# Two transposes of y moved from TensorE to transposing DMAs, and three stores to another queue, in a linear-attention and channel-mix kernel

## The chip, the core and the metric

The kernel runs on one core of a Trainium2 chip. The metric is the device time of one execution in microseconds; for several runs it is their median. The kernel's order of instructions is written out by hand, so each engine works through a fixed list.

## The reference

For each of 8 batches and 8 heads, with 576 tokens and 64 columns a head, linear attention without a mask is computed and normed, and its output goes through a channel mix with a shift by one token:

```python
kv = np.einsum('bhsd,bhse->bhde', k, v)
out = np.einsum('bhsd,bhde->bhse', q, kv)
rms = np.sqrt(np.mean(out * out, axis=-1, keepdims=True) + 1e-06)
x = (out / rms * g_norm)            # heads side by side: [8, 576, 512]
...
x_prev = np.concatenate([zeros, x[:, :-1, :]], axis=1)
xk = mu_k * x + (1.0 - mu_k) * x_prev
xr = mu_r * x + (1.0 - mu_r) * x_prev
k = np.maximum(xk @ w_k, 0.0)       # 512 -> 1024
v = k * k @ w_v                     # 1024 -> 512
r = 1.0 / (1.0 + np.exp(-(xr @ w_r)))
return (r * v)
```

Inputs and output are float32; the kernel works in bfloat16 with float32 sums.

## The kernel before, in words

Batches are counted from 0 in the code (a or b = 0 to 7); batch seven is a = 6, batch eight a = 7. The work of a batch is cut into small steps, each a short word in ORDER (lines 18 to 110), and the words are run in that order. A word names a step and its arguments: `K.6.5.1'=0` is step K for batch 6, chunk 5, half 1; a stroke puts its copy on DVE in place of ScalarE; the digits behind the equals sign are the PSUM banks that it takes. A bank is free again when the instruction that reads it last has been written down in the order. Each engine runs its own instructions in the order of the words and waits only for what they need. ORDER has eight periods; period p holds mostly the channel mix of batch p and the attention of the next one or two.

The steps that matter here, in the order in which a batch a passes through them:

- `ld` (lines 189 to 194): POOL issues the load of q, k or v with a cast to bfloat16.
- `kv`, `kvo`, `kvs`: k times v on TensorE, copies of it to SBUF, and a copy with the partition halves swapped.
- `qd` (lines 302 to 305): from a = 4 on, one transposing DMA on SP's queue turns q, 18 blocks of 128x128. Before that `qt` turns q on TensorE.
- `u`: q times kv into PSUM, in three parts. `sq` (ScalarE), `red` and eight `nw` (DVE) make the reciprocal root of the mean square by two Newton steps.
- `mul` (lines 393 to 397): DVE multiplies u by it and writes y, tokens in partitions. Five per batch; part 2 is the first group of 64 tokens, which stands alone ("group zero").
- `x0` and `x` (lines 413 to 429): TensorE turns y in 4 and 32 pieces (line 411). `x0o` and `xo` (lines 419, 431) copy the result from PSUM to xT with the factor g (`move`, lines 399 to 403), two copies each. xT has two buffers, one for even and one for odd a; a row of it is 64 columns of the token before and then the 576 tokens, 640 columns for each of four head pairs.
- `wrap` (line 567) fills the 64 columns ahead of the tokens, since tokens stand in a permuted order of nine groups. `dif` (line 571) subtracts the shifted x, four `sc` per mix (lines 577 and 579) multiply by mu, two `add` per mix (line 594) give xk (`add.a.0`) and xr (`add.a.1`).
- `K` (lines 603 to 622): four matmuls of 288 columns on xk, then the relu copy to an rt buffer, of which there are seven. `ks` squares an rt buffer of both halves into sqk. 16 K and 8 ks per batch.
- `R` (lines 626 to 632): four matmuls of 512 columns on xr and a sigmoid on ScalarE. `V` (lines 634 to 640): the product with w_v for a tile of 128 tokens in two parts of four matmuls. Tiles are counted over a pair of batches, nine to a pair; `V.7.5` is tile 5 of the last pair.
- `fin` (lines 650 to 655): DVE multiplies the V product from PSUM by the sigmoid into one of seven output buffers, and both halves of 64 partitions are stored by two DMAs on SP's queue. The last tile, 8 of the last pair, is done in two halves of columns, `L.1` and `L.0` (lines 642 to 648); there the first store is on SP's queue and the second on ScalarE's.

A store or a transposing DMA waits, beside its data, until the transfer eight before it has landed, because eight semaphores go round. SP's queue holds the q transposes and all stores but two.

Of the kernel before, what the change touches and what calls it, by code (L numbers as in the profile page):

```python
# [45 lines left out]
    red.2.0.5 nw.2.0.1 ksp.1.1.0.2 ld.0.4 R.1.5=5 Kp.1.1.5=7 nw.2.1.2 nw.2.2.3 ksp.1.1.4.6 nw.2.3.4 nw.2.4.5
    nw.2.5.6 R.1.8=1 nw.2.6.7 nw.2.7.8 mul.2.1.0 Kp.1.1.7=5 mul.2.1.1 mul.2.2.0 mul.2.0.0 R.1.6=7 V.1.4.0=2
    x0.2=16 mul.2.0.1 x0o.2.1 x0o.2.0 ksp.1.1.6.8 qt.3.1=35 kv.3=74 x.2.0.4=61 V.1.5.0=0 xo.2.0.4.0' xo.2.0.4.1
    V.1.5.1 ld.1.4 wrap.2 V.1.4.1 dif.2 kvo.3.1 V.1.7.0=6 sc.2.0.1' sc.2.0.0' sc.2.0.2 sc.2.0.3 sc.2.1.0
    add.2.0.0 sc.2.1.2' V.1.7.1 V.1.6.0=1 sc.2.1.3' qto.3.1.1 add.2.0.1 V.1.6.1 kvo.3.0'  # L50
# [13 lines left out]
    K.3.4.0'=7 fin.2.0 sc.3.1.1 u.4.0=41 u.4.1=53 sc.3.1.2' sq.4.0.1 sq.4.1.0 ld.2.7 u.4.2=2 K.3.1.0=0 sq.4.0.0
    add.3.1.0 sq.4.2.0 K.3.1.1'=7 K.3.5.1=6 red.4.5.9 K.3.0.1=0 K.3.5.0'=7 sq.4.1.1 red.4.0.5 K.3.3.1=6
    add.3.1.1 nw.4.0.1 nw.4.1.2 nw.4.2.3 K.3.0.0=0 K.3.2.0=7 kv.5=60 kvo.5.0 nw.4.3.4 nw.4.4.5 kvo.5.1 K.3.7.0=7
    nw.4.5.6 K.3.2.1=6 nw.4.6.7 ks.3.0 nw.4.7.8 kvs.5.1 mul.4.1.1 ks.3.2' R.3.7=0 mul.4.0.0 V.2.3.0=7 mul.4.2.0
    mul.4.0.1 ks.3.5 K.3.4.1=6 K.3.6.1=0 V.2.3.1 kvs.5.0' ks.3.1' ld.0.7 ks.3.4 K.3.7.1=3 K.3.3.0=6 mul.4.1.0
    R.3.6=4 K.3.6.0=2 ks.3.3 fin.2.3 x0.4=01 u.5.2=3 x0o.4.1' ks.3.7' x0o.4.0' ks.3.6 x.4.0.4=56 xo.4.0.4.1'
# [7 lines left out]
    K.4.3.1=5 mul.5.2.0 V.3.8.0=7 K.4.0.1=0 K.4.5.1=1 qd.6 sc.4.1.3' ks.4.3' add.4.1.1 ks.4.0 x.5.0.4=62
    xo.5.0.4.0 xo.5.0.4.1' kv.6=43 x0.5=50 K.4.5.0=1 add.4.1.0 wrap.5 kvo.6.1' K.4.2.0'=2 x0o.5.0 ks.4.7'
    x0o.5.1 ks.4.5' kvo.6.0 ks.4.2 R.4.1=6 K.4.6.1=3 kvs.6.1' R.4.0=1 dif.5 sc.5.0.1 sc.5.0.2 K.4.4.1=5 kvs.6.0
    K.4.4.0'=2 sc.5.0.3' sc.5.0.0 V.3.8.1 fin.3.8 sc.5.1.1' V.4.0.0=0 R.4.2=4 u.6.1=63 ks.4.6' sq.6.1.1 ks.4.4'  # L80
    add.5.0.1 add.5.0.0 u.6.2=1 sq.6.2.0 u.6.0=25 sq.6.0.0 V.4.0.1 fin.4.0 sq.6.0.1 qd.7 sq.6.1.0
    """,
    """
    K.5.7.0=7 R.4.3=4 K.5.5.1=0 K.5.3.1=7 red.6.5.9 red.6.0.5 nw.6.0.1 K.5.5.0=4 K.5.1.1=0 K.5.2.0=7 nw.6.1.2
    nw.6.2.3 nw.6.3.4 K.5.2.1=4 nw.6.4.5 nw.6.5.6 K.5.7.1'=0 K.5.1.0'=7 V.4.1.0=4 nw.6.6.7 K.5.4.1=0 nw.6.7.8
    mul.6.2.0 sc.5.1.0 V.4.1.1 mul.6.0.1 ks.5.1 mul.6.1.0 V.4.3.0=7 sc.5.1.2 x0.6=10 mul.6.0.0 mul.6.1.1
    sc.5.1.3' kv.7=56 ks.5.2' x0o.6.0' add.5.1.0 x0o.6.1' kvo.7.1 kvo.7.0 x.6.0.4=23 xo.6.0.4.1 add.5.1.1
    xo.6.0.4.0 kvs.7.0 wrap.6 K.5.0.0=6 dif.6 K.5.4.0=5 fin.4.1 kvs.7.1 K.5.6.1=1 sc.6.0.0' K.5.0.1'=0 K.5.6.0=3
# [16 lines left out]
    K.7.3.1'=2 V.6.2.1 V.6.3.0=6 V.6.0.0=4 fin.5.7 ks.7.3' fin.6.2 R.6.0=1 K.7.7.1=2 V.6.1.0=3 ks.7.7' fin.5.5
    K.7.5.1'=5 ks.7.1 K.7.0.1=1 R.6.3=2 K.7.6.1=7 fin.5.8 add.7.1.0 ks.7.2' ks.7.0 V.6.1.1 V.6.3.1 V.7.7.0=5
    sc.7.1.2 add.7.1.1 ks.7.5 fin.6.1 V.7.4.0=1 R.7.6=0 R.7.5=2 ks.7.6 R.7.7=7 V.7.6.0=3 R.7.4=0 fin.6.3 V.7.4.1
    V.6.0.1 V.7.5.0=6 fin.7.4 V.7.6.1 V.7.5.1 V.7.7.1 fin.6.0 R.7.8=2 fin.7.6 fin.7.5 fin.7.7 L.1=7 L.0=0 wm.1=1
# [10 lines left out]
def kernel(  # L119
# [272 lines left out]

    def mult(a, part, i):
        y, rs, (t0, n) = mine(a, "y", [128, NRG, NHP, HD], BF16), at[a]["rs"], TILES[part]
        g = rg(t0, n, i) if n else slice(0, 1)
        DVE.tensor_mul(out=y[:, g], in0=give(("u", a, part, i)),  # L396
                       in1=rs[:, g].unsqueeze(3).to_broadcast([128, max(n, 1), NHP, HD]))
# [252 lines left out]
    def finish(b, t, key, c=slice(0, C), queues=(nc.sync, nc.sync)):  # L650
        o = work.tile([128, c.stop - c.start], FP32, tag="out", name="out_sb", bufs=7)
        DVE.tensor_mul(out=o, in0=give(key), in1=sig[b, t][:, c])  # L652
        for i in range(2):
            bb, j = b - b % 2 + (2 * t + i) // G, (2 * t + i) % G
            queues[i].dma_start(out=out[bb].rearrange("(p j) c -> j p c", j=G)[j, :, c], in_=o[half(i), :])
# [35 lines left out]
    def part_square(b, j, f0, f1, eng):  # L691
# [101 lines left out]
```

## Time and profile before

| what | value |
|---|---|
| three runs of the kernel before | 202.69, 200.93, 203.99 us; median 202.69 |
| profiled execution, own time | 201.74 us |
| its span | 200.0 us |
| granted clock of TensorE | 0.997 |
| instructions in the span | 6027 |
| matmuls of line 411 (turning y) | 252, 6.4 us busy |
| HBM read and written | 33.56 MB and 9.44 MB |

The page of the profile gives busy times of each engine (PE is TensorE's matmuls, PEld its weight loads, DVE VectorE, ACT ScalarE, POOL GpSimd, SP SyncE, which issues DMAs), shares of the chain of work that ended last, and groups of instructions by line. "ps_x" is the PSUM tile of the turned y, "ps_km" that of K, "ps_r" of R, "ps_v" of V; "m" is the product with mu, "dx" the difference, "rt" the relu, "sqk" its square, "out_sb" an output buffer. In the views of one line, three numbers with strokes between them are the least, the median and the greatest duration in nanoseconds. A queue is written SPq or ACTq.

### The profile page before, as it was taken

The page shows a single profiled execution, that of the slowest core. Times are in us where ns is not written, and L with a number is a line of the kernel's source. Part 1 is how long each engine was busy: PE and PEld are TensorE (multiplying, and loading weights), DVE is VectorE, ACT ScalarE, POOL GpSimd, SP SyncE. Part 2 cuts the span into 40 slices and gives each one's busy share as a digit, 9 for nine tenths or more (in the row PEclk, how much of TensorE's full clock was granted, in tenths as well). Part 3 has the DMA queues.
Part 4 walks back from the last instruction along what each step waited for, and adds up shares of the span by engine and source line. Part 5 has one row for each costly group of instructions (what it writes and reads, how often), then busy time and mean ns, then how long its engine had stood idle before and what let it go on. Part 6 is the DMA issues. An engine that isn't in the chain of part 4 may idle for free.

```text
span 200.0 us, 6027 instructions
## 1 busy us (share of the span) xinstructions
PE 190.9 (95%) x2523; PEld 114.0 (57%) x2523; DVE 158.4 (79%) x344; ACT 140.3 (70%) x289; POOL 27.2 (14%) x44
## 2 busy tenths in 40 slices
PE   7789999999999999999999999999999999999990
PEld 2446744665455764476645665766565556554450
DVE  1499997998978999999999998898889973763250
ACT  3397975989956996788893899959986955075210
POOL 7854342003000400412000000000000000000000
PEclk9999999999999999999999999999999999999998
DMA  6999999999994899999999902530330020465284
GB/s 216 213 206 207 201 206 209 207 233 227 252 209 81 134 214 164 231 247 272 212 227 219 185 3 52 116 61 0 86 77 3 0 52 3 91 140 116 49 179 113
DMA packets 30767, 29.56 MB, mean 148 GB/s; under 512 B 11148, under 2 KB 25748, under 8 KB 30740
## 3 DMA queue, kind: packets, MB, share of 16 engines
q0 software_dynamic: 14912, 16.19, 48.6%
q1 hardware_dynamic: 15668, 12.85, 27.6%
q8 instruction: 20, 0.33, 0.6%
q10 hardware_dynamic: 160, 0.13, 0.2%
q14 instruction: 7, 0.06, 0.1%
HBM read 33.56 MB, written 9.44 MB: 215 GB/s over the span
## 4 chain that ended last, share of the span: by engine, by line
PE 88%; DMA 4%; DVE 2%; POOL 1%; issue 1%; ACT 1%; DVEq 0%; POOLq 0%
PE ps_v L639 30%; PE ps_km L607 29%; PE ps_r L629 16%; DMA rt<-in_v_dram 4%; PE ps_x L411 3%; PE ps_km L679 2%; PE ps_kv L290 2%; PE ps_u L319 2%; PE ps_qt L333 1%; PE ps_v L647 1%; PE ps_u L355 1%; PE ps_warm L264 1%; POOL q L183 1%; ACT sq L521 1%; DVE sqk L615 1%
## 5 line engine op out<-in xcount | busy, mean ns | idle before, releaser
L607 PE MATMUL ps_km<-xk,wk_sb 128*128 128x288 bf16 (+3 forms) x480 | 66.7, 285 | 0.0
L639 PE MATMUL ps_v<-wv_sb,sqk 128*128 128x512 bf16 x280 | 66.4, 379 | 0.3
L607 PEld LDWEIGHTS <-wk_sb 128*128 128x128 bf16 x480 | 45.4, 98 | 18.3 <-issue 0.2
L599 ACT ACTIVATE rt<-ps_km 128x288 bf16<-128x288 f32 (+3 forms) x87 | 35.9, 428 | 14.4 <-PE ps_km L607 12.3
L639 PEld LDWEIGHTS <-sqk 128*128 128x128 bf16 x280 | 26.7, 98 | 28.8 <-DVE sqk L615 0.4
L632 ACT ACTIVATE sig<-ps_r 128x512 bf16<-128x512 f32 x36 | 21.3, 596 | 21.3 <-PE ps_r L629 21.3
L629 PE MATMUL ps_r<-wr_sb,xr 128*128 128x512 bf16 x144 | 35.8, 379 | 0.0
L652 DVE TENSOR_TENSOR out_sb<-ps_v,sig 128x512 f32<-128x512 f32 (+1 forms) x37 | 24.6, 671 | 9.5 <-ACT sig L632 5.7
L577 ACT ACTIVATE m<-dx,cols 128x576 bf16<-128x576 bf16 (+1 forms) x34 | 24.8, 763 | 1.8 <-DVE dx L571 1.7
L613 ACT ACTIVATE sqk<-rt 128x576 bf16<-128x576 bf16 (+2 forms) x32 | 22.1, 710 | 0.1
L601 DVE TENSOR_SCALAR rt<-ps_km 128x288 bf16<-128x288 f32 (+3 forms) x33 | 15.4, 471 | 8.0 <-PE ps_km L607 7.8
L629 PEld LDWEIGHTS <-xr 128*128 128x128 bf16 x144 | 13.8, 98 | 13.3
L396 DVE TENSOR_TENSOR y<-ps_u,rs 128x512 bf16<-128x512 f32 (+1 forms) x30 | 17.2, 630 | 0.3
L364 DVE TENSOR_REDUCE ss<-sq 128x16 f32<-128x1024 bf16 (+1 forms) x12 | 15.9, 1346 | 0.3 <-ACT sq L360 0.3
L360 ACT ACTIVATE sq<-ps_u 128x512 bf16<-128x512 f32 (+1 forms) x30 | 14.4, 560 | 1.4 <-PE ps_u L319 1.4
L615 DVE TENSOR_TENSOR sqk<-rt 128x576 bf16<-128x576 bf16 (+4 forms) x25 | 12.4, 509 | 2.4 <-ACT rt L599 2.1
L594 DVE TENSOR_TENSOR xr<-m,xT 128x1152 bf16<-128x1152 bf16 x16 | 12.0, 751 | 1.7 <-ACT m L577 1.5
L401 ACT ACTIVATE xT<-ps_x,cols 128x1024 bf16<-128x1024 bf16 (+3 forms) x17 | 10.4, 648 | 3.5 <-PE ps_x L411 3.3
L571 DVE TENSOR_TENSOR dx<-xT 128x2304 bf16<-128x2304 bf16 (+5 forms) x13 | 11.6, 895 | 1.0 <-ACT xT L401 0.5
L594 DVE TENSOR_TENSOR xk<-m,xT 128x1152 bf16<-128x1152 bf16 (+2 forms) x16 | 10.8, 698 | 0.1
L579 DVE TENSOR_SCALAR m<-dx,cols 128x576 bf16<-128x576 bf16 (+3 forms) x32 | 10.4, 354 | 0.2
L403 DVE TENSOR_SCALAR xT<-ps_x,cols 128x128 bf16<-128x128 bf16 (+3 forms) x19 | 8.0, 438 | 2.1 <-PE ps_x L411 1.9
(87 smaller groups left out, 153.9 us busy)
## 6 DMA issues: line engine op xcount, KB each, us to landing
out_dram<-out_sb SPq DMA_DIRECT2D x70, 128.0 KB, 2.5
sq<-in_k_dram POOLq DMA_DIRECT2D x3, 576.0 KB, 14.6
qT<-in_v_dram POOLq DMA_DIRECT2D x3, 576.0 KB, 15.1
q<-in_q_dram POOLq DMA_DIRECT2D x3, 576.0 KB, 12.6
in_q<-in_q_dram POOLq DMA_DIRECT2D x3, 576.0 KB, 12.4
in_v<-in_v_dram POOLq DMA_DIRECT2D x3, 576.0 KB, 16.4
in_k<-in_k_dram POOLq DMA_DIRECT2D x3, 576.0 KB, 14.3
wk_sb<-in_moe_w_k_dram POOLq DMA_DIRECT2D x2, 512.0 KB, 9.8
```

Source lines behind the costliest of these rows:

```text
L364: DVE.tensor_reduce(out=ss[:, g0:g1], in_=sq[:, g0:g1], op=ALU.add, axis=AX.X)
L396: DVE.tensor_mul(out=y[:, g], in0=give(("u", a, part, i)), in1=rs[:, g].unsqueeze(3).to_broadcast([128, max(n, 1), NHP, HD]))
L577: eng.activation(out=out_, in_=in_, func=AF.Copy, scale=mu)
L594: DVE.tensor_add(out=dst, in0=m[:, hs, c0:c1], in1=x[:, hs, c0:c1])
L599: eng.activation(out=dst, in_=ps, func=AF.Relu)
L601: eng.tensor_scalar(out=dst, in0=ps, scalar1=0.0, scalar2=None, op0=ALU.max)
L607: nc.tensor.matmul(ps[:, n, :], wk_sb[:, cc, 128 * fc:128 * fc + 128], at[b]["xk"][:, cc, c0:c1], start=(cc == 0), stop=(cc == NHP - 1))
L613: eng.activation(out=sqk[:, fcs, o:o + n], in_=src, func=AF.Square)
L629: nc.tensor.matmul(ps, xr[:, cc, 128 * t:128 * t + 128], wr_sb[:, cc, :], start=(cc == 0), stop=(cc == NHP - 1))
L632: ACT.activation(out=sig[b, t], in_=give("r"), func=AF.Sigmoid)
L639: nc.tensor.matmul(ps, sqk[:, fc, 128 * t:128 * t + 128], wv_sb[:, fc, :], start=(fc == 0), stop=(fc == NFC - 1))
L652: DVE.tensor_mul(out=o, in0=give(key), in1=sig[b, t][:, c])
```

## The change

Three things are changed. First, for a = 6 and 7 `mul` writes into a new tile yd, four head pairs by five blocks of 128 columns, and `yd` turns the whole tile by one transposing DMA on SP's queue into xT, wrap columns included: 20 blocks of 128x128. One half of yd's first block is set to zero once at the start. The multiplication of group zero becomes two instructions of 64 partitions, since its rows are all written to the upper partition half. `x`, `x0`, `xo` and `x0o` are gone for these batches; `gx` multiplies xT by g in place, in two pieces of two head pairs, both on DVE. There is one yd tile, so the multiplications of a = 7 wait until yd.6 has read it.

Second, tiles 5, 6 and 7 of the last pair are finished by `fip`, which stores the first half on SP's queue, and `sta`, which stores the second on ScalarE's.

Third, all periods but the first are in a new order, with other PSUM banks, and some copies, squares and products with mu have changed between ScalarE and DVE. In it the q transposes qd.6 and qd.7 stand earlier among the stores of SP's queue.

```diff
+    YD = (6, 7)
+    yd = const.tile([128, NHP, 1 + NHP, 128], BF16, name="yd")
+
+    def mult_rows(a, part, i):
+
+        rs, (t0, n) = at[a]["rs"], TILES[part]
+        u_, pairs = give(("u", a, part, i)), yd.rearrange("p (c i) t x -> p c i t x", i=2)
+        if n:
+            by = rs[:, rg(t0, n, i)].unsqueeze(3).to_broadcast([128, n, NHP, HD])
+            DVE.tensor_mul(out=pairs[:, :, i, 1 + t0:1 + t0 + n].rearrange("p c t x -> p t c x"), in0=u_, in1=by)
+        else:
+            for h in range(2):
+                by = rs[half(h), 0].unsqueeze(2).to_broadcast([64, NHP, HD])
+                DVE.tensor_mul(out=pairs[half(1), :, h, 0], in0=u_[half(h), 0], in1=by)
+
+    DVE.memset(yd[half(0), :, 0], 0.0)
+
+    def y_turn(a):
+
+        nc.sync.dma_start_transpose(out=xT[a % 2].rearrange("p n (t x) -> p (n t) x", x=128), in_=yd.rearrange("p n t x -> p (n t x)"))
+
+    def by_g(a, hs, eng):
+        x = xT[a % 2][:, hs, P:]
+        move(eng, x, x)
+
     def mult(a, part, i):
+        if a in YD:
+            return mult_rows(a, part, i)
...
-        for i in range(2):
-            bb, j = b - b % 2 + (2 * t + i) // G, (2 * t + i) % G
-            queues[i].dma_start(out=out[bb].rearrange("(p j) c -> j p c", j=G)[j, :, c], in_=o[half(i), :])
+        for i, q_ in enumerate(queues):
+            store(b, t, i, q_, c)
...
+        "yd": lambda eng, a: y_turn(a),
+        "gx": lambda eng, a, h: by_g(a, heads[h], eng),
...
+        "fip": lambda eng, b, t: finish(b, t, ("v", b, t), queues=(nc.sync,)),
+        "sta": lambda eng, b, t: store(b, t, 1, nc.scalar),
```

The new order of the sixth period from its middle, of the seventh, and of the eighth:

```diff
...
+    K.5.0.1=0 mul.6.1.1 sc.5.1.2 V.4.3.0=3 V.4.3.1 K.5.6.0=0 K.5.1.0=6 K.5.0.0=5 mul.6.1.0 mul.6.0.1 sc.5.1.1
+    kv.7=72 mul.6.0.0 kvo.7.0 sc.5.1.0' K.5.5.1=0 K.5.3.1=1 K.5.6.1'=6 K.5.2.0'=5 add.5.1.0 ks.5.2 kvo.7.1
+    K.5.1.1'=7 V.4.1.1 kvs.7.1 kvs.7.0' yd.6 ks.5.1 add.5.1.1 fin.4.1 K.5.7.1=0 fin.4.3 K.5.3.0=1 ks.5.5'
+    ks.5.4' K.5.7.0'=6 ks.5.3' u.7.0=52 u.7.2=7 u.7.1=04 ks.5.7' R.5.8=1 sq.7.0.0 R.5.6=3 sq.7.1.1 R.4.2=6
+    gx.6.0' sq.7.0.1 V.4.2.0=1 V.4.2.1 gx.6.1' wrap.6 ks.5.0 dif.6 sq.7.1.0 sc.6.0.2 fin.4.2 R.5.4=3 R.5.5=6
+    sc.6.0.1' sq.7.2.0 sc.6.0.0' R.5.7=1 ks.5.6 sc.6.0.3' add.6.0.0 add.6.0.1 red.7.0.5 V.5.4.0=3
     """,
     """
+    K.6.1.1=6 red.7.5.9 nw.7.0.1 nw.7.1.2 K.6.7.1=1 sc.6.1.1 nw.7.2.3 nw.7.3.4 V.5.4.1 nw.7.4.5 K.6.0.1=6
+    nw.7.5.6 V.5.6.0=1 nw.7.6.7 nw.7.7.8 mul.7.0.1 mul.7.1.1 V.5.7.0=6 V.5.7.1 mul.7.1.0 mul.7.2.0 V.5.6.1
+    sc.6.1.2 K.6.6.0=2 mul.7.0.0 yd.7 V.5.8.0=4 K.6.5.1'=0 K.6.7.0'=7 sc.6.1.3 ks.6.7' add.6.1.1 sc.6.1.0
+    add.6.1.0 V.5.8.1 K.6.2.1=2 fin.5.4 K.6.6.1'=5 K.6.2.0'=0 K.6.0.0=7 K.6.4.0'=2 K.6.3.0=3 K.6.1.0=7 K.6.5.0=5
+    ks.6.2 fin.5.7 R.6.2=0 K.6.3.1'=2 ks.6.3 R.6.1=3 fin.5.8 gx.7.1' gx.7.0' ks.6.0 V.5.5.0=6 R.6.3=7 ks.6.1'
+    wrap.7 dif.7 sc.7.0.3' fin.5.6 K.6.4.1=5 V.6.1.0=0 V.5.5.1 sc.7.1.1' sc.7.0.0 V.6.3.0=2 R.6.0=4 sc.7.0.1'
+    ks.6.6 add.7.0.0 sc.7.0.2' sc.7.1.2 add.7.0.1 V.6.2.0=3 V.6.0.0=7
     """,
     """
+    K.7.3.1'=5 K.7.5.1=1 K.7.2.1'=4 ks.6.4' ks.6.5' K.7.0.1=5 K.7.1.1=1 sc.7.1.3' K.7.0.0=4 K.7.2.0'=5
+    K.7.7.1'=1 fin.5.5 sc.7.1.0 K.7.5.0=4 K.7.6.1'=5 add.7.1.0 ks.7.0 V.6.0.1 V.6.1.1 V.6.3.1 K.7.4.1=1 ks.7.5
...
+    fin.6.0 fin.6.3 ks.7.3 R.7.7=6 R.7.4=5 V.7.7.0=1 ks.7.7' V.7.4.0=4 V.7.7.1 R.7.6=3 R.7.8=6 fip.7.7 V.7.4.1
+    sta.7.7 fin.7.4 R.7.5=7 fin.6.1 V.7.5.0=2 V.7.6.0=5 V.7.6.1 fip.7.6 sta.7.6 V.7.5.1 fip.7.5 sta.7.5 L.1=1
+    L.0=3 wm.1=6
```

More of the change, by code (lines that the diff above doesn't have):

```diff
@@ L46 @@
[L46 to L50, printed above, removed]
@@ L65 @@
[L65 to L69, printed above, removed]
@@ L77 @@
[L77 to L81, printed above, removed]
@@ L82 @@
-    """,
-    """
[L84 to L88, printed above, removed]
@@ L105 @@
[L105 to L108, printed above, removed]
+    sc.1.1.0 sc.1.0.0.0.384 sc.1.0.3.0.384 fin.0.2 sc.1.0.2.0.384' Kp.1.0.0=5 Kp.1.0.2'=0 add.1.0.0.0.384
```

76 lines of the change are left out of this document (43 added, 33 removed).

## The prediction

> **What bounds the kernel now.** I read the page first (busy times, slices, shares of the chain), then the chain of work in order of time, then the windows by stretch, then the end of the timeline with the store queues, and last the transposing DMAs that the kernel already has.
>
> ```profile
> span 200.0 us, 6027 instructions
> ...
> PE 190.9 (95%) x2523; PEld 114.0 (57%) x2523; DVE 158.4 (79%) x344; ACT 140.3 (70%) x289; POOL 27.2 (14%) x44
> ...
> POOL 7854342003000400412000000000000000000000
> ...
> PE 88%; DMA 4%; DVE 2%; POOL 1%; issue 1%; ACT 1%; DVEq 0%; POOLq 0%
> ```
>
> ```profile
> 125.30:144.20 18.90, 18.90 (x286) 12.03 (x285) 17.70 (x38) 16.05 (x35) 0.00 (x0) 1.00 0.30 63
> 144.20:163.10 18.90, 18.90 (x150) 11.41 (x149) 15.98 (x33) 14.11 (x29) 0.00 (x0) 1.00 0.19 41
> ...
> sum 156.00, PE 156.00 PEld 94.55 DVE 129.57 ACT 113.95 POOL 8.89; mean PE 22.29 PEld 13.51 DVE 18.51 ACT 16.28 POOL 1.27
> ```
>
> The second fence is the windows view, from 38.3 to 194.3 us in seven stretches (two shown, and the sum of all; behind the stretch and its length stand PE, PEld, DVE, ACT and POOL busy, the granted clock, DMA share, GB/s). TensorE is busy in 156.00 of 156.00 us at a granted clock of 1.00. So nothing is gained before 194.3 by removing a wait; there is none. Only fewer matmuls shorten this part, and a new wait lengthens it. The first part, up to about 38 us, has the same order in both kernels.
>
> The chain of work (start, length, what) shows the matmuls that go, and the end:
>
> ```profile
> 133.64 0.17 PE ps_x L411 x4
> ...
> 134.51 0.57 PE ps_x L411 x32
> ...
> 154.76 0.63 PE ps_x L411 x36
> ...
> 155.99 0.86 PE ps_v L639 x4
> 156.85 0.49 PE ps_km L607 x4
> ...
> 192.56 1.76 PE ps_v L647 x16
> ...
> 194.34 0.42 DVE out_sb L652
> ```
>
> The last product of DVE is there at 194.76, yet the span is 200.0. The end of the timeline, and the stores that are issued after 194.9, show why:
>
> ```profile
> 188.19 8.66 SPq L655 DMA_DIRECT2D out_dram<-out_sb  x12
> 193.98 1.29 ACTq L655 DMA_DIRECT2D out_dram<-out_sb  x2
> ...
> L655 SPq DMA_DIRECT2D out_dram<-out_sb x3: 546/657/846, 194.6 to 196.3; - x3
> L655 ACTq DMA_DIRECT2D out_dram<-out_sb x1: 478/478/478, 194.8 to 194.8; - x1
> DMA to landing us min/median/max: 2.0/2.4/2.8
> ```
>
> SP issues twelve stores without a pause from 188.19 to 196.85, 0.72 us each. Both halves of the last tile's last part are made at 194.76; ScalarE issues its half at 194.8, SP its own only at 196.3. The end waits for SP's backlog of 1.5 us, then 2.0 us for the landing, then 1.7 us of closing.
>
> **The change part by part.** The profiled execution took 201.74 us, 1.74 beside its span of 200.0; the sum is made against it. The median of the three runs, 202.69, is 0.95 above it.
>
> 1. Matmuls. The transposes of y leave TensorE for batches seven and eight (a = 6 and 7): 0.17 + 0.57 and 0.63 us in the chain, 36 instructions each. That is -1.37 us, and since TensorE has no gap there, the following work moves up by all of it.
>
> 2. Each of these batches gets one transposing DMA of 20 blocks of 128x128 (yd.6, yd.7) on SP's queue. The kernel already turns q with four such DMAs of 18 blocks. Those two that run after the loads have ended, and the two before:
>
> ```profile
> L305 SPq DMA_TRANSPOSE qT<-q x1: 2823/2823/2823, 110.5 to 110.5; - x1
> L305 SPq DMA_TRANSPOSE qT<-in_q x1: 2818/2818/2818, 127.3 to 127.3; - x1
> DMA to landing us min/median/max: 4.7/4.7/4.7
> ...
> L305 SPq DMA_TRANSPOSE qT<-in_q x1: 4762/4762/4762, 79.6 to 79.6; - x1
> POOL q L194: 15.0, 1
> DMA to landing us min/median/max: 9.1/9.1/9.1
> ```
>
> Alone: 2.82 us of issue on SP, 4.7 to landing. Among the loads, around 67 to 90 us: 9.1 for one, and a load that waited for the other stood 15.0. The new ones fall, as the new order lays them, near 131 and 152 us, where the DMA engines are used at 0.30 and 0.19 (the two window rows above), and no load is left: POOL, which issues the loads, is idle from 95 us on (its row of 5 us slices on the page). So I take the quiet value scaled by blocks, 20/18: 3.1 us of issue, 5.2 to landing; both ends are kept for the rivals. SP's issue time blocks only stores, and seven output buffers stand behind them.
>
> What hides 5.2 us? DVE reaches the multiplication by g (gx) only after the work that the new order puts between it and the last mul. By the rows of single forms:
>
> ```profile
> L652 DVE TENSOR_TENSOR out_sb<-ps_v,sig 128x512 f32<-128x512 f32 x35 | 23.7, 685 | 8.0 <-ACT sig L632 5.7 <-PE ps_v L639 1.7 <-DMA out_dram<-out_sb 0.3
> ...
> L601 DVE TENSOR_SCALAR rt<-ps_km 128x288 bf16<-128x288 f32 x28 | 12.5, 454 | 7.7 <-PE ps_km L607 7.5
> ...
> L594 DVE TENSOR_TENSOR xr<-m,xT 128x1152 bf16<-128x1152 bf16 x16 | 12.0, 751 | 1.7 <-ACT m L577 1.5
> ...
> L615 DVE TENSOR_TENSOR sqk<-rt 128x576 bf16<-128x576 bf16 x20 | 8.8, 452 | 2.4 <-ACT rt L599 2.1
> ...
> L579 DVE TENSOR_SCALAR m<-dx,cols 128x576 bf16<-128x576 bf16 x24 | 8.2, 368 | 0.1
> ...
> L403 DVE TENSOR_SCALAR xT<-ps_x,cols 128x1024 bf16<-128x1024 bf16 x6 | 4.5, 747 | 1.0 <-PE ps_x L411 1.0
> ...
> L396 DVE TENSOR_TENSOR y<-ps_u,rs 128x256 bf16<-128x256 f32 x6 | 2.5, 418 | 0.1
> ...
> L403 DVE TENSOR_SCALAR xT<-ps_x,cols 128x128 bf16<-128x128 bf16 x7 | 2.0, 280 | 0.3 <-PE ps_x L411 0.2
> ...
> L579 DVE TENSOR_SCALAR m<-dx,cols 128x192 bf16<-128x192 bf16 x4 | 0.8, 267 | 0.0
> ...
> L222 DVE COPY kv<-kv 64x256 bf16<-64x256 bf16 x3 | 0.7, 223 | 0.1
> ```
>
> Batch seven: one sc 0.37, four K copies 1.82, two add 1.50, one kvs 0.22, two fin 1.37, four ks 1.81: 7.1 us. Batch eight: six K copies 2.72, one ks 0.45, two add 1.50, three fin 2.06: 6.7 us. In the timeline DVE's instructions overlap by about 0.08 us, so the fourteen and twelve of them take 6.0 and 5.8; waits for K's matmuls only add to it. Cover 6.0 and 5.8, need 5.2: hidden, with 0.6 to 0.8 us to spare at least.
>
> 3. In place of the copies out of PSUM stand two gx per batch, 128x1152 each. From 192 and 576 columns (267 and 368 ns) a column costs 0.263 ns, so one gx takes 368 + 576 x 0.263 = 0.52 us, and the four 2.1. The group-zero multiplication becomes two of 64 partitions, 0.42 us more per batch if each takes what the 128x256 row takes. DVE loses four copies, three of 0.28 and one of about 0.75. Net +1.3 us in two batches, in a stretch where DVE works 15.98 of 18.90 us: room, so nothing in the sum. ScalarE loses copies; nothing.
>
> 4. The order. I laid the new words out engine by engine with these row durations. One place stops TensorE; beside the rows above it takes two of the same view for ScalarE and TensorE:
>
> ```profile
> L599 ACT ACTIVATE rt<-ps_km 128x288 bf16<-128x288 f32 x68 | 27.1, 411 | 13.4 <-PE ps_km L607 11.9
> ...
> L607 PE MATMUL ps_km<-xk,wk_sb 128*128 128x288 bf16 x384 | 53.7, 286 | 0.0
> ```
>
> K.7.0 takes the rt buffer of K.6.5 (seven buffers: 6.5, 6.2, 6.4, 6.3, 7.3, 7.5, 7.2, then 7.0), and K.6.5's square ks.6.5' is on DVE behind the copy of K.7.2.1' and ks.6.4'. From K.7.2.1's start: 0.65 until its four matmuls are through (0.49 a group, the last one 0.29 long at a pace of 0.12), copy 0.45, two squares 0.90, less overlaps 0.16, makes 1.9 with signals; then ScalarE's copy of K.7.0.1 frees bank 5 at about 2.3. TensorE would reach K.7.2.0, which takes this bank, after four groups of 0.49, at 1.96. So +0.4 us. Three more places (x of batch five, K.3, K.4.0.1 behind fin.3.7) come out between 0.1 and 0.3; the same addition gives 0.8 us in all for the old order, where the trace has none, so I count only the 0.4. Bounds: 0 and 1.2.
>
> 5. The stores. SP loses three of its last stores, 0.66 at the median of the last three and up to 0.85 each, to ScalarE. What ScalarE has behind them is one sigmoid (R.7.5) after the first, then stores only; each costs it 0.48. In the new order the tiles before the last parts are 7.6 and 7.5, one store each on SP, 0.87 us apart (one V group); the four stores before them (7.4 and 6.1) are ready some 2.7 us earlier and are through by then. So SP is free when the last part is made and issues at the same time as ScalarE: 194.8 instead of 196.3 on the old clock, -1.5 us. Bounds: -0.8 (SP still late by one store) and -1.6.
>
> Sum: -1.37 + 0.4 - 1.5 = -2.5, so 199.3 us against the profiled 201.74, and 200.2 against the median. One execution and three runs lie between 200.93 and 203.99; midway between profiled time and median, 202.2, I forecast 199.8.
>
> **The rivals.**
>
> A: the transposes land late, slower. Place: gx.6 and gx.7, with wrap, dif, sc, add and the first K group queued behind them on DVE. Price: each microsecond beyond the cover of 6.0 and 5.8 stops TensorE for one. The gain of 2.5 is gone when both land 1.2 us beyond it, at 7.1; at the loaded 9.1 x 20/18 = 10.1 us the excess is 4.1 + 4.3, and the time 199.8 + 8.4 = 208.2. Against it: no load is left then, and 4.7 was measured twice in this state. The Trainium skill, page "VectorE: DVE Perf Modes", section "The three transpose paths", gives 1309 ns for a 128x128 bf16 block through the DMA crossbar against 390 on TensorE, and advises TensorE where PSUM will do. An estimate from that page, 20 blocks one after another, is 26 us to landing, some 20 beyond the cover for each batch, about 240 us in all. The trace disagrees: 4.7 us for 18 blocks is 0.26 per block.
>
> B: the tail does not shorten, since the landing of ScalarE's later stores, or a store that waits for an earlier landing (2.0 to 2.8 us), ends last. Then only -1.37 + 0.4 remains: 202.2 - 1.0 = 201.2. For it: SP's stores took up to 0.85 us and wait for earlier landings in turn. Against it: ScalarE's own last store, issued 1.5 us ahead of SP's, was not what the end waited for. The Trainium skill, page "DMA: Bandwidth & Descriptors", section "Issuing engines are not separate DMA queues", says that issuing from several engines saves only the sequencer's time to start a transfer, usually small beside the transfer; by that usual case the time would be this rival's, while the trace has SP's issues, back to back, as what ends last.
>
> C: the new order's small waits all come true (1.2) while the tail gains its least (0.8): -1.37 + 1.2 - 0.8 = -1.0, also 201.2. A different cause for the same time.
>
> D: no new wait at all and the whole tail: -1.37 - 1.6 = -3.0, 199.2, and 198.0 if the runs lie as low as the lowest shown (200.93).
>
> **How the numbers follow.** The forecast with D as its favourable edge 0.76, A 0.06, B 0.11, C 0.07. The predicted time is that of the forecast, 199.8. Low 198.0 is D on the lowest base; high 202.4 takes in B and C with about a microsecond of spread between runs; A is left out. A measurement of this kernel tells about 2% from no change, 4.05 us: faster than 198.6 needs D and low runs, 0.12; slower than 206.7 needs A with some 3.5 us of excess in each batch, 0.06; the rest 0.82.
>
> **What would show it.** Right: no row for line 411 after batch six (252 - 72 = 180 transposes left), landings near 5.2 us for two DMAs of xT, DVE's idle time before gx not released by them, SP's last store issued within 0.2 us of ScalarE's, and the end of TensorE near 193.3. Wrong: a wait of DVE for "DMA xT", a matmul waiting for ks.6.5 or its copy well beyond 0.4 us, or a span that ends 3.7 us after a store of SP which again stood in line.

## The result and the profile after

| | before | after |
|---|---|---|
| median of 20 runs each, side by side | 202.06 us | 199.57 us |
| ratio after to before, 95% interval | | 0.9902 (0.9874 to 0.9930) |
| profiled execution | 201.74 us | 199.54 us |
| its span | 200.0 us | 197.8 us |

The changed kernel is about 1% faster, which is 2.0 us (1.4 to 2.5) of 202.06 and less than the 2% of the prediction's bound. The ratio leaves out the executions that were over 1.5% slower than their kernel's fastest, of which both kernels have some; the medians of all 20 lie 2.5 us apart. The forecast was 199.8 us with a range of 198.0 to 202.4.

The page of the changed kernel has these rows against those shown of before (line numbers of the changed kernel are 28 higher behind the new functions: 607 became 635, 639 became 667; the store's line 655 became 688):

```profile
span 197.8 us, 5867 instructions
...
PE 188.6 (95%) x2427; PEld 112.7 (57%) x2451; DVE 159.3 (81%) x348; ACT 135.8 (69%) x284; POOL 26.8 (14%) x44
...
L635 PE MATMUL ps_km<-xk,wk_sb 128*128 128x288 bf16 (+3 forms) x480 | 65.0, 285 | 0.0
```

There are 2451 weight loads and 2427 matmuls where before both were 2523. The 72 transposes are gone; another 24 matmuls are missing from the records, so TensorE's busy times are not compared below, only when it reaches a place. ScalarE loses 4.5 us, DVE gains 0.9. The last column of the third row, the idle time ahead of K's products, is 0.0: none of them waited.

The chain of work and the end of it:

```profile
168.84 4.90 PE ps_km L635 x40
...
191.35 1.76 PE ps_v L675 x16
193.14 0.42 DVE out_sb L680
```

TensorE's last product ends at 191.35 + 1.76 = 193.11, where it was 192.56 + 1.76 = 194.32: 1.21 us sooner. From the start of DVE's last product to the end of the span it is 197.8 - 193.14 = 4.7 us, where it was 200.0 - 194.34 = 5.7: 1.0 us shorter. Both together are the 2.2 us between the spans.

### The profile page after: what moved, and what is told of

It is laid out like the page before. It is cut to its first block, busy times and chain, and to the rows that moved or that the text cites. A ratio compares the mean times of both kernels' runs of the same rounds, so it can differ in the third digit from the quotient of the medians.

```text
span 197.8 us, 5867 instructions
## 1 busy us (share of the span) xinstructions
PE 188.6 (95%) x2427; PEld 112.7 (57%) x2451; DVE 159.3 (81%) x348; ACT 135.8 (69%) x284; POOL 26.8 (14%) x44
## 4 chain that ended last, share of the span: by engine, by line
PE 88%; DMA 4%; issue 2%; DVE 2%; POOL 1%; ACT 1%; DVEq 0%; POOLq 0%
PE ps_v L667 29%; PE ps_km L635 29%; PE ps_r L657 16%; DMA rt<-in_v_dram 4%; PE ps_km L712 2%; PE ps_kv L291 2%; PE ps_x L439 2%; PE ps_u L320 2%; PE ps_qt L334 1%; PE ps_u L356 1%; PE ps_v L675 1%; POOL q L184 1%; PE ps_warm L265 1%; ACT sq L549 1%; DVE sqk L643 1%
## 5 line engine op out<-in xcount | busy, mean ns | idle before, releaser
L667 PE MATMUL ps_v<-wv_sb,sqk 128*128 128x512 bf16 x266 | 65.0, 379 | 1.4 <-issue 0.6
L635 PE MATMUL ps_km<-xk,wk_sb 128*128 128x288 bf16 (+3 forms) x480 | 65.0, 285 | 0.0
L627 ACT ACTIVATE rt<-ps_km 128x288 bf16<-128x288 f32 (+3 forms) x95 | 39.2, 425 | 22.7 <-PE ps_km L635 19.5
L657 PE MATMUL ps_r<-wr_sb,xr 128*128 128x512 bf16 x136 | 34.9, 379 | 0.6 <-issue 0.2
L605 ACT ACTIVATE m<-dx,cols 128x576 bf16<-128x576 bf16 (+1 forms) x31 | 22.5, 764 | 2.0 <-DVE dx L599 2.0
L641 ACT ACTIVATE sqk<-rt 128x576 bf16<-128x576 bf16 (+2 forms) x30 | 21.1, 717 | 1.6 <-DVE rt L629 1.5
L629 DVE TENSOR_SCALAR rt<-ps_km 128x288 bf16<-128x288 f32 (+3 forms) x25 | 11.8, 477 | 9.9 <-PE ps_km L635 9.7
L424 DVE TENSOR_TENSOR y<-ps_u,rs 128x512 bf16<-128x512 f32 (+1 forms) x20 | 11.4, 629 | 0.2
L265 PE MATMUL ps_warm<-zeros 128*128 128x512 bf16 x22 | 8.4, 517 | 1.5 <-DVE eps L228 1.2
L429 ACT ACTIVATE xT<-ps_x,cols 128x256 bf16<-128x256 bf16 (+3 forms) x13 | 7.0, 563 | 2.9 <-PE ps_x L439 2.9
## 6 DMA issues: line engine op xcount, KB each, us to landing
wk_sb<-in_moe_w_k_dram POOLq DMA_DIRECT2D x2, 512.0 KB, 10.3
```

Source lines behind the costliest of these rows:

```text
L605: eng.activation(out=out_, in_=in_, func=AF.Copy, scale=mu)
L627: eng.activation(out=dst, in_=ps, func=AF.Relu)
L635: nc.tensor.matmul(ps[:, n, :], wk_sb[:, cc, 128 * fc:128 * fc + 128], at[b]["xk"][:, cc, c0:c1], start=(cc == 0), stop=(cc == NHP - 1))
L641: eng.activation(out=sqk[:, fcs, o:o + n], in_=src, func=AF.Square)
L657: nc.tensor.matmul(ps, xr[:, cc, 128 * t:128 * t + 128], wr_sb[:, cc, :], start=(cc == 0), stop=(cc == NHP - 1))
L667: nc.tensor.matmul(ps, sqk[:, fc, 128 * t:128 * t + 128], wv_sb[:, fc, :], start=(fc == 0), stop=(fc == NFC - 1))
```

## The experiments

Each ratio is to the kernel before, run beside it, with a 95% interval.

### The stores back on one queue, new order

```diff
-    fip.7.7 V.7.4.1 sta.7.7 fin.7.4 ... fip.7.6 sta.7.6 V.7.5.1 fip.7.5 sta.7.5
+    fin.7.7 V.7.4.1 fin.7.4 ... fin.7.6 V.7.5.1 fin.7.5
```

> The changed kernel with both stores of tiles 7.7, 7.6 and 7.5 on SP's queue again. Theory (the tail shortens because SP has no backlog when the last part is made; part of that comes from the new order, which brings 7.7 and 7.4 forward): after 191.30 SP has four stores of 7.6 and 7.5 at 0.47 to 0.59 us before the two of the last parts, so its last store is issued some 0.6 us later than the 193.6 of the changed kernel; ratio to the kernel before 0.993. Rival 1 (the two queues are worth the whole 1.0 us by which the tail shrank): 0.995 or more. Rival 2 (transfers, not issues, end last): no change, 0.990.

Measured: 0.9918 (0.9885 to 0.9952), between the two and not separable from the changed kernel's 0.9902. The store rows from 188 us on and the last product:

```profile
L688 SPq DMA_DIRECT2D out_dram<-out_sb x10: 466/570/591, 187.7 to 194.3; - x10
...
DMA to landing us min/median/max: 2.3/2.4/2.4
```

```profile
192.99 0.42 DVE L680 TENSOR_TENSOR out_sb<-ps_v,sig 128x256 f32<-128x256 f32 x1 [0.45 <-PE ps_v L675]
```

SP issues its last store at 194.3, 1.3 us behind the last product; before it was 2.0 us (196.3 against 194.34). So the new order alone, which brings whole tiles forward, takes 0.7 us from SP's backlog without the second queue. From the start of the last product to the end of the span it is 197.8 - 192.99 = 4.8 us, where it was 5.7 before and is 4.7 in the changed kernel. Of the 1.0 us by which the end became shorter, 0.85 is there with the stores on SP's queue, which speaks against rival 1.

### The stores on two queues, old order

Two placements. The first has the last sigmoid (R.7.8) behind two of the moved stores on ScalarE, the second has it ahead of them:

```diff
-    fin.6.0 R.7.8=2 fin.7.6 fin.7.5 fin.7.7 L.1=7
+    fin.6.0 fip.7.6 sta.7.6 fip.7.5 sta.7.5 R.7.8=2 fip.7.7 sta.7.7 L.1=7
```

> The kernel before, its order kept, with the second stores of tiles 7.6, 7.5 and 7.7 on ScalarE's queue; TensorE's order is the same. Theory: SP's last store is issued at about 194.8 in place of 196.3, but lands later after the issue, as in the changed kernel; net -1.0 us, ratio 0.995. Rival (the transfers end last): 1.000.

```diff
-    fin.6.0 R.7.8=2 fin.7.6 fin.7.5 fin.7.7 L.1=7
+    fin.6.0 R.7.8=2 fip.7.6 sta.7.6 fip.7.5 sta.7.5 fip.7.7 sta.7.7 L.1=7
```

> The order of the kernel before, with the second stores of the three last whole tiles on ScalarE's queue, as in the first of this kind (ratio 0.997), but with the last sigmoid ahead of these stores on ScalarE, so that none of them delays it. Theory (the stores' queue is worth what the prediction counted, 0.8 to 1.5 us, and the sigmoid behind the stores took it back): ratio 0.993 to 0.996. Rival (stores issued at one time on two queues take longer each, so that the queue matters little by itself): ratio 0.997 to 1.000.

Measured: 0.9973 (0.9942 to 1.0003) and 0.9973 (0.9938 to 1.0009), 0.5 us each, neither separable from no change by itself. The timeline of the first from 192.7 us on:

```profile
192.77 1.50 ACTq L660 DMA_DIRECT2D out_dram<-out_sb  x1
...
194.31 0.60 ACT L632 ACTIVATE sig<-ps_r 128x512 bf16<-128x512 f32 x1 [5.99 <-DMA out_dram<-out_sb]
194.40 2.40 ACTq L660 DMA_DIRECT2D out_dram<-out_sb  x3
...
195.52 0.42 DVE L652 TENSOR_TENSOR out_sb<-ps_v,sig 128x256 f32<-128x256 f32 x1 [0.15 <-PE ps_v L647]
```

Its store rows from 188 us on:

```profile
L660 SPq DMA_DIRECT2D out_dram<-out_sb x9: 467/546/1503, 189.4 to 196.0; - x9
...
L660 ACTq DMA_DIRECT2D out_dram<-out_sb x5: 498/613/1496, 191.9 to 196.0; - x5
```

One store's issue took 1.50 us on ScalarE, and the sigmoid stood behind it until 194.31. The last product of this execution, 195.52, waited for TensorE all the same, which had lost 1.4 us in one wait between 80 and 100 us, where this kernel is still the same as the one before. Both queues issue their last store 0.5 us behind the last product, and the span ends 4.6 us behind it, where it was 5.7: here the backlog is gone in the old order too. The second placement, store rows from 188 us on and then the timeline:

```profile
L660 SPq DMA_DIRECT2D out_dram<-out_sb x9: 466/467/588, 188.6 to 195.2; - x9
...
L660 ACTq DMA_DIRECT2D out_dram<-out_sb x5: 551/561/757, 193.0 to 195.8; - x5
```

```profile
193.04 3.53 ACTq L660 DMA_DIRECT2D out_dram<-out_sb  x5
...
194.72 0.42 DVE L652 TENSOR_TENSOR out_sb<-ps_v,sig 128x256 f32<-128x256 f32 x1 [0.39 <-PE ps_v L647]
```

Here nothing holds the sigmoid, but ScalarE now has five stores in line from 193.04 to 196.57, and the last is issued at 195.8. From the last product to the end it is 5.9 us: the backlog has changed queues. So by the ratios the second queue is worth about 0.5 us in the old order, or nothing, half of what the first expectation's theory had and within the second's rival (0.997 to 1.000). The two traces don't agree on why: the first placement ends as soon behind its last product as the changed kernel does, the second does not. What each placement is worth over many executions stays open.

### The transposing DMAs in the old order

The two DMAs and the multiplications by g stand where the transposes and their copies stood:

```diff
-    x0.6=10 mul.6.0.0 mul.6.1.1 ... x0o.6.0' ... x0o.6.1' ... x.6.0.4=23 xo.6.0.4.1 ... xo.6.0.4.0
+    mul.6.0.0 mul.6.1.1 yd.6 ... gx.6.0' gx.6.1'
...
-    x.7.0.4=41 x0.7=27 ... x0o.7.0' xo.7.0.4.0' xo.7.0.4.1 ... x0o.7.1
+    yd.7 ... gx.7.0' gx.7.1'
```

> The kernel before, its order kept, with y of batches seven and eight turned by the transposing DMA; yd behind the last mul, both gx where the copies from PSUM stood. Theory (the transfer is free only under cover): the multiplications end at 134.2, landing 5.3 later at 139.5, gx, wrap and dif behind it end some 3.5 us later than the 138.6 of before; TensorE loses about 3.5 and 3 us and gains 1.37: 207 us, ratio 1.025. Rival (a transposing DMA costs nothing wherever it stands): -1.37 us, 0.993.

Measured: 1.0414 (1.0380 to 1.0447), 8.4 us slower. DVE's wait for the landings and then the two longest waits of TensorE, from 60 us on (us in total, times, longest); the execution shown took 212.87 us, some 2.5 more than the median of its four, so the rows show better where the waits are than what they cost:

```profile
DVE xT L430 <- DMA xT<-yd: 7.3, 2, 4.4
```

```profile
PE ps_km L634 <- DVE xk L621: 4.7, 1, 4.7
PE ps_u L319 <- DVE out_sb L679: 2.1, 1, 2.1
```

The mechanism is the theory's: without work laid between the last mul and gx, DVE stands for the landing, and TensorE behind it, 6.8 us in all where the theory had 6.5. The time rose by more, 8.4 in place of 5.1. The theory had no term for the granted clock, which falls to half after each of these two pauses (last section): by an estimate from the rows there that costs some 1.6 us each, about the difference. The change therefore needs its order; the DMAs alone lose time in the way that rival A describes.

### TensorE's transposes in the new order

The changed kernel with x0, x and their copies back for a = 6 and 7, in three layouts of the PSUM banks. The first takes the nearest free banks; the second and third take those longest idle, copy at once and rename the banks that follow. Of the second, without the banks renamed behind these places:

```diff
-    YD = (6, 7)
+    YD = ()
...
-    kvs.7.0' yd.6 ks.5.1 add.5.1.1 ...
+    kvs.7.0' x0.6=20 x.6.0.4=16 ks.5.1 x0o.6.0' x0o.6.1' xo.6.0.4.0 xo.6.0.4.1' add.5.1.1 ...
...
-    R.6.2=0 K.6.3.1'=2 ks.6.3 R.6.1=3 fin.5.8 gx.7.1' gx.7.0' ...
+    R.6.2=2 K.6.3.1'=4 x0.7=03 x.7.0.4=76 ks.6.3 xo.7.0.4.1 x0o.7.0' x0o.7.1' xo.7.0.4.0' R.6.1=0 fin.5.8 ...
```

> The changed kernel, its order and its stores kept, with y of batches seven and eight turned on TensorE and copied from PSUM as before. Theory: 72 matmuls are back on a TensorE without gaps: +1.37 us, ratio 0.997. Rival (the new order alone is the gain, the matmuls fall into gaps): 0.990.

> Order and stores of the changed kernel, with y of the last two batches turned on TensorE again. Its first form came out at 1.015, with 1.9 us of TensorE's wait on one ScalarE copy of batch eight's turned y and a late u of batch eight, because the turned y took accumulators that were wanted again at once. Here the turned y takes the accumulators that have been idle longest, its copies come at once, and the accumulators after it are renamed. Theory (the transposes are worth their own 1.37 us of matmuls and nothing else): end of TensorE some 1.4 us later than in the changed kernel, no wait on a copy over 0.5 us, ratio 0.997 (0.995 to 0.999). Rival 1 (the order alone gave the gain): ratio 0.990. Rival 2 (four turned accumulators and four copies can't be had beside the work of that stretch, whichever banks they take): waits stay, ratio 1.005 or more.

> As the run before with TensorE's transposes in the changed order, with the accumulators of batch seven's stretch dealt out again: that run still had 0.85 us of wait where a product with wk took an accumulator that a copy of the turned y had not left, and 0.28 us behind another copy, and came out at 1.004. Theory (the transposes are worth their matmuls, 0.7 us for each batch, and every wait comes from the accumulators that the turned y takes and can be dealt away): no wait over 0.3 us, ratio 0.996 to 0.999. Rival (four more accumulators and their copies on ScalarE and VectorE can't be placed in this order without a wait somewhere): a new wait in place of the old, ratio 1.002 or more. Rival (the order alone gave the gain): 0.990.

Measured: 1.0146 (1.0130 to 1.0162), 1.0037 (1.0006 to 1.0069) and 1.0056 (1.0016 to 1.0096). The longest wait of TensorE from 38 us on in each, in this order:

```profile
PE ps_v L667 <- ACT xT L429: 1.9, 1, 1.9
```

```profile
PE ps_km L635 <- DVE xT L431: 0.9, 1, 0.9
```

```profile
PE ps_km L635 <- DVE out_sb L680: 1.5, 1, 1.5
```

All three missed the theory's 0.996 to 0.999. Each time a wait for a bank went away, another came: behind ScalarE's copy of the turned y, behind DVE's, behind a tile's product. The best layout is 2.7 us behind the changed kernel (0.0135 of 202), twice the 1.37 us of matmuls. Apart from the transposes TensorE's weight loads come in the same order as in the changed kernel, so the traces can be laid side by side, load by load. The three run level with it, within 0.3 us, up to 135 us, and fall behind after that only at the two turnings and at waits. A turning puts TensorE back by some 1.0 to 1.3 us, 2.1 to 2.3 for both; the waits add 1.4 to 2.5, and TensorE ends 3.5 to 4.8 us later. So the order alone is not the gain, and even without the waits the turnings would cost more here than their 1.37. What is shown is that three layouts by hand did not fit; that no layout fits is not. The kernel before, whose order was laid for the transposes, has no wait of TensorE from 38 us on.

### How much cover the landing has

One or two more transposing DMAs of the same tile, into spare tiles, ahead of each real one:

```diff
     def y_turn(a):
+        for s_ in spare:
+            nc.sync.dma_start_transpose(out=s_, in_=yd.rearrange("p n t x -> p (n t x)"))
         nc.sync.dma_start_transpose(out=xT[a % 2]...
```

> The changed kernel with one further transposing DMA of the same tile into a spare tile ahead of each of the two, so that the real one is issued 2.9 us and lands about 3 us later, 8.3 us after it could start. Theory by the measured cover (8.2 us from the last product to batch seven's product with g, 7.8 us from the issue to batch eight's): VectorE waits 0.2 to 0.5 us for each, and the time rises by at most that: ratio 0.990 to 0.995. Rival (the cover of 6.0 and 5.8 us that the prediction read is all there is): VectorE waits 2.3 and 2.5 us and TensorE behind it, ratio 1.005 to 1.015.

> The same with two further transposing DMAs ahead of each: the real one lands some 11 us after it could start. Theory by the measured cover: VectorE waits about 3 us for each, none of it hidden for batch seven only if the scores are urgent: rise of 3 to 7 us, ratio 1.005 to 1.025. Rival (a landing later than the cover by 3 us is taken up by work that VectorE and TensorE do in between): ratio 0.990 to 0.995. Rival from the prediction (cover 6.0 and 5.8, every us beyond it on the path): rise of 10 us, ratio 1.04.

Measured: 1.0017 (0.9982 to 1.0052) with one, 1.0327 (1.0245 to 1.0410) with two. The first lies between what was expected of theory and rival. Its real DMAs, their landing, and what waited:

```profile
L416 SPq DMA_TRANSPOSE xT<-yd x2: 3129/3154/3180, 135.9 to 159.0; - x2
...
DMA to landing us min/median/max: 6.1/6.3/6.6
```

```profile
DVE xT L434 <- DMA xT<-yd: 3.9, 2, 2.1
```

```profile
PE ps_v L670 <- DVE sqk L646: 1.2, 2, 1.0
...
PE ps_r L660 <- DVE out_sb L683: 1.1, 1, 1.1
```

For batch seven the real DMA is issued at 135.9 in place of 132.1 and lands 6.6 us later at most, 142.5. In the changed kernel DVE starts that batch's gx at 140.30. The wait is 2.1, close to the difference of 2.2: what the landing goes beyond the place where DVE wants it, DVE stands. The theory's cover was right; for batch seven the landing came 10.3 us after it could start and not 8.3, since the first DMA took up to 3.6 us of issue and the second up to 6.6 to land. Of DVE's 3.9 us TensorE waits for 2.1, and the time rises by 2.3 (1.0017 against 0.9902). With two ahead:

```profile
DVE xT L434 <- DMA xT<-yd: 8.0, 2, 4.6
```

```profile
PE ps_r L660 <- DVE out_sb L683: 3.7, 1, 3.7
PE ps_v L670 <- DVE sqk L646: 2.7, 2, 2.5
```

By the ratios that is 8.6 us over the changed kernel, from four executions, between the theory's 1.025 and the last rival's 1.04. The span of the one shown is 10.0 us longer than the changed kernel's, of which 3.7 and 2.5 are these waits; most of the rest is in the last section.

### One more turning by DMA

The q of a = 3 is turned by a transposing DMA too, in place of 72 transposes (two words of 36; the expectation below counts one of them) and four copies. In the first kernel it is issued behind the stores of tile 3 of the first pair:

```diff
-    QD = 4
+    QD = 3
...
-    qt.3.1=16 ... qto.3.1.0' ... qto.3.1.1 ... qt.3.0=63 ... qto.3.0.1' qto.3.0.0'
+    fin.0.3 qd.3 ... kvs.3.0' kvs.3.1'
```

In the second qd.3 moves, and in the third two of K's products go ahead of u.3 besides:

```diff
-    fin.0.1 Kp.1.1.4=6 add.1.1.1 R.0.3=2 Kp.1.1.6=5 fin.0.3 qd.3
+    fin.0.1 qd.3 Kp.1.1.4=6 add.1.1.1 R.0.3=2 Kp.1.1.6=5 fin.0.3
...
-    K.2.6.1=2 K.2.2.1=0 ld.2.5 ld.0.5 u.3.0=31 ... K.2.1.0=0 K.2.3.0=7
+    K.2.6.1=2 K.2.2.1=0 K.2.1.0=6 K.2.3.0=3 ld.2.5 ld.0.5 u.3.0=51 ...
```

> The changed kernel with q of the batch numbered 3 turned by a transposing DMA as that of 4 to 7 is, instead of 36 transposes on TensorE and four copies; its products with k then go by block, as those of 4 to 7. Theory (what leaves TensorE leaves the time, where the DMA lands ahead): TensorE loses 0.8 us of transposes and 0.1 us of products, ratio 0.985 to 0.987. Rival (this DMA is issued among the loads, where the one of batch 6 took 6.2 us to issue, lands late, and TensorE or ScalarE waits for it): 0.990 or more. Second rival (the stretch at 50 to 65 us isn't set by TensorE): 0.990.

> The kernel that turns q of the batch numbered 3 by a transposing DMA, with that DMA issued 2.5 us sooner, behind the stores of the tile before. At its first place TensorE lost 0.95 us of work and waited 1.37 us for the landing, ratio 0.988. Theory (the landing moves with the issue, and then 0.9 us leave the time): no wait of TensorE on this DMA, ratio 0.984 to 0.987. Rival (the DMA shares the engines with the loads in flight and lands when they do, however early it is issued): TensorE waits 1 us or more again, ratio 0.988 or more.

> As the run before with q of the batch numbered 3 turned by the DMA, with two of batch three's products with wk (0.98 us of TensorE) put ahead of the products that need the turned q, and the accumulators after them renamed. In the run before TensorE waited 1.04 us there, since the DMA landed at 67.2 us of its span wherever it was issued. Theory (the landing is fixed by the loads in flight, so the use has to be moved and not the issue): TensorE's wait 0.3 us or less, its end 0.5 us or more ahead of the changed kernel's, ratio 0.982 to 0.985. Rival (batch three's normalization comes 1 us later and something behind it waits in turn): ratio 0.986 or more.

Measured: 0.9879 (0.9827 to 0.9931), 0.9858 (0.9809 to 0.9908) and 0.9883 (0.9863 to 0.9904). The DMA's row and who waited for it (us, times) in the first, then the same of the second:

```profile
L306 SPq DMA_TRANSPOSE qT<-in_q x1: 10452/10452/10452, 50.4 to 50.4; - x1
...
  PE ps_u L320: 1.4, 1
```

```profile
L306 SPq DMA_TRANSPOSE qT<-in_q x1: 9875/9875/9875, 48.1 to 48.1; - x1
...
  PE ps_u L320: 1.0, 1
```

Issued 2.3 us sooner, it spared TensorE 0.4 us of waiting. That is the rival's mechanism, a landing that hardly moves with the issue, though this kernel's ratio of 0.9858 is nearer the theory's number. That the loads in flight set the landing is argued from this and not shown. With the use put later that wait is gone, but the time is not:

```profile
PE ps_km L635 <- ACT rt L627: 0.6, 1, 0.6
PE ps_r L657 <- issue: 0.3, 1, 0.3
```

New waits take its place, as the last rival said. The third run's ratio is the rival's (0.986 or more). All three are as fast as the changed kernel or a little faster, and no interval stands clear of the changed kernel's; a version that beats it was not shown.

## Why the prediction was right

**The bound.** TensorE without a gap until 194.3, then the stores: both parts moved the time. A longer landing of the transposing DMA cost nothing until it came to its place on DVE, then over half of what it was late by (2.3 us of time for DVE's 3.9 of waiting).

**Step 1, the matmuls (-1.37).** Right in the sum: 180 transposes are left on the turning line, 252 - 72, and TensorE ends 1.21 us sooner. Both orders are free of waits, each with its own way of turning. Putting the transposes back into the new order costs 2.7 us or more, of which the turnings by themselves are 2.1 to 2.3 and the rest is waits for banks and copies. So that taking them away is worth at least the 1.37 there is shown; that it was worth just that in the change from the old order to the new is argued from a TensorE without gaps in both.

**Step 2, the landing (5.2).** Right. The two DMAs, and gx in place, by the views of the line and the tile:

```profile
L413 SPq DMA_TRANSPOSE xT<-yd x2: 2957/3354/3752, 132.1 to 153.8; - x2
...
DMA to landing us min/median/max: 4.9/5.3/5.7
```

```profile
L431 DVE TENSOR_SCALAR xT<-xT,cols x4: 508/512/517, 140.3 to 162.0; 128x1152 bf16<-128x1152 bf16 x4
```

Among DVE's waits none is for "DMA xT". Batch seven's DMA starts at 132.1 and its gx at 140.3, so the cover is 8.2 us, not the 6.0 that was called the least: DVE had waits for K's products in between, which the prediction named and did not count. For batch eight it is 7.8 (153.8 and 161.6), not 5.8. Hence rival A was some 2 us further off than it looked. The runs with DMAs ahead show that its mechanism is real. Its price, one microsecond of TensorE for each beyond the cover, was too high for a small excess: with one DMA ahead 3.9 us of DVE's waits became 2.1 of TensorE's, with two 8.0 became 6.2, and there the clock came on top. The Trainium skill's 1309 ns for each 128x128 block on the crossbar ("VectorE: DVE Perf Modes", "The three transpose paths") stays off: 5.3 us for 20 blocks is 0.27 each.

**Step 3 (gx 0.52, no cost).** Right: 0.512 measured in the row above.

**Step 4 (the order, +0.4).** Wrong. TensorE doesn't wait at K.7.2.0: the chain's row at 168.84 holds forty of K's matmuls without a break. The premise was that K.7.0 takes the rt buffer of K.6.5, whose square ends late on DVE. The timeline of DVE and ScalarE there:

```profile
170.72 0.82 DVE L643 TENSOR_TENSOR sqk<-rt 128x576 bf16<-128x576 bf16 x2
```

```profile
170.83 1.39 ACT L627 ACTIVATE rt<-ps_km 128x288 bf16<-128x288 f32 x3 [0.51 <-PE ps_km L635]
```

The first of ScalarE's three copies is K.7.0.1's. It runs at 170.83, before DVE has finished the two squares ks.6.4 and ks.6.5 at 171.54, so K.7.0 has another buffer. That the seven buffers go strictly in turn was an assumption, and the 0.4 hung on it.

**Step 5 (the stores, -1.5).** The cause, SP's backlog, is right. The term was mis-sized, the end is 1.0 us shorter, and most of it is not the work of the second queue. The stores of the changed kernel from 190 us on:

```profile
L688 SPq DMA_DIRECT2D out_dram<-out_sb x5: 466/467/587, 189.6 to 193.6; - x5
...
L688 ACTq DMA_DIRECT2D out_dram<-out_sb x4: 499/550/759, 191.3 to 193.6; - x4
...
DMA to landing us min/median/max: 2.3/2.6/3.0
```

Both queues issue their last store at 193.6, as predicted, 0.5 us behind the last product instead of 2.0. That is the 1.5 us. But the span ends 4.2 us after this issue, where it was 3.7. By kernel, from the rows shown and the spans:

| kernel | last product | last store issued | span ends | product to issue | issue to end |
|---|---|---|---|---|---|
| before | 194.34 | 196.3 | 200.0 | 2.0 | 3.7 |
| new order, stores on SP | 192.99 | 194.3 | 197.8 | 1.3 | 3.5 |
| after | 193.14 | 193.6 | 197.8 | 0.5 | 4.2 |
| old order, stores moved, sigmoid behind | 195.52 | 196.0 | 200.1 | 0.5 | 4.1 |
| old order, stores moved, sigmoid ahead | 194.72 | 195.8 | 200.6 | 1.1 | 4.8 |

In the three rows in which whole tiles' stores go out on both queues at once, the last store is issued sooner behind the last product and the end follows that issue 0.4 us or more later than before. In the changed kernel that gives back about a third of the 1.5. The landing times in the traces show where it goes: the last landing comes 2.0 us after the last issue in the first two rows and 2.4 to 3.1 in the other three, and what follows the last landing is 1.5 to 1.7 us in all five. The prediction took the landing as fixed. About half of the backlog went with the order and not with the queue (first row against second). In the new order the second queue brings 0.15 us by the time from the last product to the end (4.81 and 4.66) and 0.3 us by the ratios (0.9918 and 0.9902, not separable); in the old order it is 0.5 us by the ratios. The page "DMA: Bandwidth & Descriptors" of the Trainium skill says, under "Issuing engines are not separate DMA queues", that a second issuing engine saves only the time to start a transfer and that this is usually small beside the transfer. These runs agree.

The misses of steps 4 and 5 offset each other in part: without a wait TensorE ends at -1.21 instead of -0.97, and the end gives -1.0 instead of -1.5. The -2.2 that they add up to, against -2.5 forecast, is the difference of the two profiled executions. That the total came so near is partly luck: one term stood for a wait that isn't there, and another put down to the queue what the order did. Rival B had part of the truth, the longer landing, without being the case.

## What to carry to other kernels

When a transfer replaces engine work, find the place where its result is first wanted, count waits into the cover as well as work, and lay the order so that the place comes later than the landing. While loads were in flight, moving the issue hardly moved the landing here; moving the use took the wait away, but not the time. Work that leaves a full engine takes its accumulators and copies along: putting it back cost more here than its instructions. The backlog of stores at this kernel's end was cut mostly by making results earlier; of what the second queue saved at the issue, part was lost at the landing.

## What the runs showed of the hardware

A pause of TensorE can cost more than itself. In the run with two DMAs ahead, the windows around its two waits show the granted clock (the number before the last two):

```profile
148.50:150.00 1.50, 1.50 (x4) 0.50 0.38 81
150.00:152.00 2.00, 2.00 (x9) 0.65 0.32 71
152.00:154.00 2.00, 2.00 (x15) 1.00 0.00 0
...
171.50:173.00 1.50, 1.20 (x3) 0.63 0.91 204
173.00:175.00 2.00, 2.00 (x6) 0.50 0.27 59
175.00:177.00 2.00, 2.00 (x10) 0.92 0.60 131
```

After the pauses of 3.7 and 2.5 us, which end at 148.4 and 171.8, the rows make 3.0 and 3.4 us at a clock of 0.50. That is some 1.5 us more for each; with the waits of 6.2 us it is most of the 10.0 us by which the span grew. The run with the DMAs in the old order shows the same after its pauses of 2.1 us (up to 145.4) and 4.7 us (up to 173.5):

```profile
146.00:148.00 2.00, 1.95 (x5) 0.63 0.60 136
148.00:150.00 2.00, 2.00 (x6) 0.52 0.07 18
...
173.50:175.00 1.50, 1.50 (x8) 0.61 0.40 87
175.00:177.00 2.00, 2.00 (x7) 0.50 0.00 0
```

After shorter pauses the clock stayed at 1.00: 1.1 us in the run with one DMA ahead, 1.5 in the third layout with TensorE's transposes, and 1.9 in the first, whose window from 38.3 to 198 us is:

```profile
38.30:198.00 159.70, 155.07 (x1987) 1.00 0.69 131
```

The Trainium skill ("TensorE: Matmul & The Clock Gate", "Part 1: The HAM clock gate") gives the half clock after an idle window of about 3.4 us. The pauses of 3.7 and 4.7 us agree; those of 2.5 and 2.1 were shorter (the last lies among small products of u), and there the measurement decides.

A transposing DMA of 18 blocks took 9.9 to 10.5 us of SP's issue time among the loads, against 2.82 in quiet.
